# Two interleaved transformer layers on one core: the norm of the one-layer steps behind bank evictions, and the last two feed-forwards' gates by 128-row weights loaded anew

## The chip, the cores and the metric

The kernel runs on one core of one Trainium2 chip. The metric is the device time of one execution in microseconds. TensorE is called PE below, VectorE DVE, ScalarE ACT, GpSimdE POOL; SP is the engine whose queue issues nearly all DMAs.

## The reference, cut to what matters

```python
# x: 1 x 2048 x 448 (bf16); 16 heads of 256; segments of 32 tokens behind 8 memory rows; F = 1792
def A(x, mem):                        # memory-augmented attention, segment after segment
    for s in range(64):
        h = concat([mem, x[:, 32*s:32*s+32]])            # 40 rows
        q, k, v = h @ Wq, h @ Wk, h @ Wv
        p = softmax(mask(q @ k.T * 256 ** -0.5))
        o = (p @ v) @ Wo
        mem = o[:, :8]; outs.append(o[:, 8:])            # the next segment needs this memory
    return concat(outs)

def B(x, W_gate, W_up, W_down):       # gated feed-forward
    return (relu(x @ W_gate) * (x @ W_up)) @ W_down

x = x + A(layernorm(x)); x = x + B(layernorm(x))         # layer 1
x = x + A(layernorm(x)); x = x + B(layernorm(x))         # layer 2, the same weights
```

The segments of a layer are a chain through the memory; the two layers overlap with a lag.

## The kernel before, in words

At the start the kernel fuses the attention weights: `A_sb`, `A3`, `A3z` hold the query-key product, `B_sb` the value-output product. The first dimension of `A_sb` that is sliced is the 128-row part `kd` (0 to 2), the second the half `hf` of the heads (0, 1). Then come 68 steps, `step(g, ff)`. Layer 1 is at segment g, layer 2 at segment g - 4. So steps 0 to 3 have only layer 1 (one chain), steps 4 to 63 both, steps 64 to 67 only layer 2.

Within a step PE runs in an order written out by hand (`in_order` ties every matmul to the one before it): `pairs` and `wide` make the query-key projections of a bank (`prj`), `close_bank` and `leave_bank` copy a bank out to `TQ` or `TZ` on DVE or ACT, `scores_m` and `scores_x` make scores (`Sm`, `Sx`) for memory and token rows, the `weights_` functions the softmax (`mx`, `se`, `ssum`, `rs`, into `PM`, `PX`), `weigh_m`, `weigh_m_rows` and `weigh_x` weigh the rows (`ya`, `yb`, `ym`, `y` into `Y` and `Z`), and `project_out` and `project_tail` project them (`ox`, `o`). `hk` are the transposed rows of the step. Other engines are ordered by a scheduler from the program's text; `tc.keep_in_program_order` pins an instruction to its place in the text among the pinned ones of its engine. There are seven PSUM banks under the tag `ps`, and one under `ox`.

Every odd step from 3 on also carries a feed-forward, `Feed(i)`, of 64 tokens of layer 1 and 64 of layer 2 (block i). It goes through `residual` (adds the attention's output to `xa` and takes the row statistics: `stats`, `mv` on DVE, then `rstd` on POOL), `norm` (`xn`, two DVE instructions that need `rstd`), `xposed` (four transposes into `tps`, one DVE copy to `xT`) and `xposed_rest` (two ACT copies that put the other halves' rows into `xT`), `gate_up(u)` for u = 0 to 6, `down`, and `leave` (the last sum and the output's DMA). Only half of a block is filled in the first (`Feed(0)`, in step 3) and in the last two: `Feed(32)` in step 67, and `end = Feed(33)`, which follows it at the end of the kernel.

`gate_up` keeps the weights in `Wgu_sb` with rows of `W_up` in partitions 0 to 63 and rows of `W_gate` in 64 to 127; the 448 rows make 7 passes of 64. One matmul of 64 rows for up (`ups`) and one for gate (`gps`) run side by side. Each u makes two tiles of 128 columns; ACT copies `ups` to `ut` (two buffers), DVE makes `hh = max(gps, 0) * ut`. `down` multiplies `hh` by `Wd_sb` into `dps`. In the last step the tokens are projected by `project_tokens` (tile `ot`) and added by `add_tokens` (tiles `sums0`, `sums1`), and the last down is made in two column halves (`down_halves`), so that the first half's output leaves while the second is made.

`load_behind` issues a DMA on SP that waits for the last PE instruction in the text so far; `load_piece` uses it to fill `Wgu_sb` and `Wd_sb` early in the run. `mm` (line 83), `tr` (line 86) and `evac` (lines 102, 103) record most matmuls, transposes and copies, so many rows of the profile have these lines, and go by tiles.

Of the kernel before, what the change touches and what calls it, by code (L numbers as in the profile page):

```python
# [54 lines left out]
def build_kernel(ctx, tc, A_x, A_mem0, A_Wq, A_Wk, A_Wv, A_Wo, B_W_gate, B_W_up, B_W_down, out,  # L55
# [16 lines left out]
    last_pe = [None]  # L72
# [20 lines left out]
    def load_behind(dst, src):  # L93
# [4 lines left out]
        return d  # L98

# [342 lines left out]
    hh = main.tile([P, FT, 128], BF, name="hh")  # L442
    part = main.tile([P, 2, DM], F32, name="part")


    class Feed:


        def __init__(self, i):
# [6 lines left out]
            self.both = self.first and self.second  # L456

# [13 lines left out]
        def xposed(self):  # L471
            tps = transpose_tokens(self.xn)
            nc.vector.tensor_copy(xT[:, 0:4, self.n], tps[:, :, self.n])
            return tps

        def xposed_rest(self, tps):
            for r in range(2):
                nc.scalar.copy(xT[ROWS[r], 4:NPASS, self.n], tps[ROWS[1 - r], 0:3, self.n])
# [15 lines left out]

        def down(self):
            i = self.i
            dps = self.dps = [psum.tile([P, 512], F32, tag="ps", name="dps") for _ in range(1 if self.both else 2)]
            for f in range(FT):
                if self.both:
                    mm(dps[0][:, 0:DM], hh[:, f, :], Wd_sb[:, f, :], start=(f == 0), stop=(f == FT - 1))  # L500
                else:
                    mm(dps[f % 2][ROWS[f % 2], 0:DM], hh[:, f, self.n], Wd_sb[:, f, :], start=(f < 2), stop=(f >= FT - 2))
# [7 lines left out]
        def sum_up(self, dst, o):  # L510
# [5 lines left out]
            nc.scalar.copy(part[n, 1, :], self.dps[1 - mine][ROWS[1 - mine], 0:DM])  # L516
# [5 lines left out]
        def down_halves(self):  # L522
            n = self.n
            dps = [[psum.tile([P, 512], F32, tag="ps", name="dps") for _ in range(2)] for _ in range(2)]
            for h, fs in ((0, range(12)), (1, range(6)), (0, range(12, FT)), (1, range(6, FT))):
                d = slice(HALF * h, HALF * h + HALF)
                for f in fs:
                    mm(dps[h][f % 2][ROWS[f % 2], 0:HALF], hh[:, f, n], Wd_sb[:, f, d], start=(f < 2), stop=(f >= FT - 2))
# [130 lines left out]
    def weights_end(se, dst, tag):  # L659
# [7 lines left out]
        nc.vector.tensor_tensor(dst[:, :, 0:L], se, rs.unsqueeze(2).to_broadcast([P, n, L]), op=ALU.mult)  # L667
# [29 lines left out]
    def step(g, ff):  # L697
# [190 lines left out]
        if last:  # L888
            nc.gpsimd.tensor_copy(hb[ROWS[0], j, 4 * HI:4 * HI + 104], hb[ROWS[0], j, 3 * HI:3 * HI + 104])
            begun = [begin_x(hf, scores_x(hf)) for hf in range(2)]  # L890
# [5 lines left out]
            end = Feed(ff.i + 1)  # L896
            project_tokens(0, o[0], 0, 0, NT)
# [3 lines left out]
            px1 = flipped_rows([(PX[1], 2)], "x1")  # L901
            project_tokens(0, o[0], 1, 14, NT)
# [185 lines left out]
```

## Time and profile before

| | before |
|---|---|
| time, median of 3 runs | 1538.44 us (1534.18 to 1540.04) |
| the profiled execution | 1537.08 us, span 1535.3 us |
| PE busy | 1514.6 us, 99% of the span |
| DVE busy | 1048.2 us, 68% |
| ACT busy | 806.3 us, 53% |
| granted PE clock | 0.999 |
| DMA | 33.08 MB; queues at work in the first 5% of the span, mean 22 GB/s over all of it |

The page's shares are taken over the whole span. Steps 3, 65, 66 and 67 take some 70 us of it, so a share says little of them; the timeline of each does. In a timeline a line has the start and the length in us, the engine, the source line, the operation, its output and inputs, the shape and the number merged; in brackets the idle time of that engine before it, and the instruction whose end ended it. Lengths of matmuls overlap, since they are pipelined: the time from one start to the next is their pace.

### The profile page before, as it was taken

How to read it: one execution, taken by the hardware profiler on the slowest of the kernel's cores; microseconds unless marked ns; L12 is line 12 of the kernel's file. 1: busy time of each engine (PE TensorE's matmuls, PEld its weight loads, DVE VectorE, ACT ScalarE, POOL GpSimd, SP SyncE). 2: the span in 40 equal slices, each digit the busy share in tenths (PEclk: the TensorE clock that was granted, in tenths of full speed). 3: DMA queues.
4: the chain of work that ended last, by engine and by line, in shares of the span. 5: the costliest groups of instructions: out<-in, count | busy, mean ns of one | idle time of the engine just before them, and what ended most of it. 6: DMA issues, size and time to landing. Idle time of an engine off the chain costs nothing.

```text
span 1535.3 us, 97340 instructions
## 1 busy us (share of the span) xinstructions
PE 1514.6 (99%) x44691; PEld 1400.5 (91%) x44691; DVE 1048.2 (68%) x3793; ACT 806.3 (53%) x2364; POOL 163.6 (11%) x309
## 2 busy tenths in 40 slices
PE   9999999999999999999999999999999999999998
PEld 6588999999999999999999999999999999999987
DVE  6756767766667667666676676666766776667665
ACT  5645554555455555554555555545555555455534
POOL 4000111011001110110011101100111011011100
PEclk9999999999999999999999999999999999999999
DMA  8910000000000000000000000000000000000000
GB/s 251 243 35 9 9 10 10 5 10 10 10 10 10 10 10 4 10 10 10 10 10 10 9 4 11 10 10 10 10 10 10 5 10 10 10 9 7 7 7 7
DMA packets 29546, 33.08 MB, mean 22 GB/s; under 512 B 3464, under 2 KB 28240, under 8 KB 29136
## 3 DMA queue, kind: packets, MB, share of 16 engines
q1 hardware_dynamic: 28928, 26.74, 6.5%
q8 instruction: 349, 5.72, 1.5%
q14 instruction: 61, 0.50, 0.1%
q10 hardware_dynamic: 144, 0.11, 0.1%
q0 software_dynamic: 64, 0.01, 0.0%
HBM read 23.18 MB, written 1.84 MB: 16 GB/s over the span
## 4 chain that ended last, share of the span: by engine, by line
PE 95%; DVE 2%; DMA 1%; ACT 1%; issue 1%; POOL 0%; DVEq 0%; ACTq 0%
PE prj L83 31%; PE ox L83 25%; PE ups L83 10%; PE dps L83 6%; PE o L83 5%; PE y L83 4%; PE Sx L83 3%; PE aps L83 1%; PE Sm L83 1%; PE pps L86 1%; PE gps L83 1%; PE bps L83 1%; PE tps L86 1%; PE flip L86 1%; PE ym L83 1%; PE tpw L86 1%
## 5 line engine op out<-in xcount | busy, mean ns | idle before, releaser
L83 PEld LDWEIGHTS <-B_sb 128*128 128x128 bf16 (+1 forms) x15008 | 482.6, 103 | 25.5 <-issue 17.9
L83 PE MATMUL prj<-hT,A_sb 128*128 128x80 bf16 (+1 forms) x11256 | 429.1, 200 | 0.0
L83 PEld LDWEIGHTS <-A_sb 128*128 128x128 bf16 x11256 | 406.3, 100 | 7.5
L83 PE MATMUL ox<-Y,B_sb 128*128 128x80 bf16 (+2 forms) x5712 | 218.4, 200 | 0.7 <-ACT Y L765 0.3
L83 PE MATMUL ox<-Z,B_sb 128*128 128x80 bf16 (+1 forms) x5544 | 213.0, 200 | 0.8 <-ACT Z L765 0.8
L83 PE MATMUL ups<-xT,Wgu_sb 64*128 64x128 bf16 (+1 forms) x3332 | 190.0, 213 | 1.5 <-DVE hh L492 0.7
L83 PE MATMUL gps<-xT,Wgu_sb 64*128 64x128 bf16 (+1 forms) x3332 | 190.2, 213 | 1.3 <-issue 0.7
L83 PEld LDWEIGHTS <-Wgu_sb 64*128 64x128 bf16 x6664 | 178.0, 94 | 6.1 <-issue 3.8
L102 ACT CAST TQ<-prj 128x480 bf16<-128x480 f32 (+3 forms) x414 | 175.8, 469 | 13.6 <-PE prj L83 2.0
L103 DVE CAST TQ<-prj 128x480 bf16<-128x480 f32 (+3 forms) x353 | 137.8, 425 | 62.6 <-PE prj L83 62.6
L102 ACT CAST Z<-y 64x128 bf16<-64x128 f32 (+2 forms) x263 | 91.3, 373 | 139.9 <-PE y L83 88.1
L102 ACT CAST TZ<-prj 64x320 bf16<-64x320 f32 (+2 forms) x292 | 110.8, 387 | 78.0 <-PE prj L83 74.6
L491 ACT CAST ut<-ups 128x256 bf16<-128x256 f32 (+1 forms) x238 | 85.3, 359 | 83.0 <-PE gps L83 62.8
L492 DVE SCALAR_TENSOR_TENSOR hh<-gps,ut 128x256 bf16<-128x256 f32 (+1 forms) x238 | 94.1, 407 | 46.9 <-ACT ut L491 34.5
L102 ACT CAST Y<-y 128x512 bf16<-128x512 f32 (+1 forms) x252 | 87.4, 375 | 61.7 <-DVE Y L103 58.7
L102 ACT COPY hT<-tps 128x256 bf16<-128x256 bf16 (+1 forms) x32 | 11.8, 369 | 192.8 <-DVE hT L103 192.8
L103 DVE CAST Y<-y 128x512 bf16<-128x512 f32 (+1 forms) x252 | 102.4, 417 | 9.2 <-ACT Y L102 3.9
L103 DVE CAST Z<-y 64x128 bf16<-64x128 f32 (+2 forms) x257 | 101.7, 417 | 9.7 <-ACT Z L102 4.6
L656 ACT ACTIVATE se<-se 128x80 f32<-128x80 f32 (+2 forms) x270 | 69.6, 292 | 45.2 <-DVE se L655 43.2
L83 PE MATMUL dps<-Wd_sb,hh 128*128 128x448 bf16 (+2 forms) x490 | 90.9, 348 | 0.0
L664 DVE TENSOR_REDUCE ssum<-se 128x2 f32<-128x80 f32 (+2 forms) x270 | 68.3, 267 | 33.0 <-ACT se L656 31.9
L192 POOL TENSOR_SCALAR rstd<-mv 128x1 f32<-128x1 f32 x67 | 15.2, 226 | 696.4 <-DVE mv L190 696.3
(141 smaller groups left out, 2211.6 us busy)
## 6 DMA issues: line engine op xcount, KB each, us to landing
wo<-in_A_Wo_dram SPq DMA_DIRECT2D x8, 448.0 KB, 7.7
Wgu_sb<-in_A_Wq_dram SPq DMA_DIRECT2D x8, 384.0 KB, 5.8
Wgu_sb<-in_A_Wk_dram SPq DMA_DIRECT2D x8, 384.0 KB, 5.8
nat<-in_A_Wv_dram SPq DMA_DIRECT2D x8, 384.0 KB, 5.5
xa<-in_A_x_dram SPq DMA_DIRECT2D x32, 56.0 KB, 2.2
xa<-xp SPq DMA_DIRECT2D x32, 56.0 KB, 1.9
out_dram<-xa SPq DMA_DIRECT2D x31, 56.0 KB, 2.0
xp<-in_A_x_dram SPq DMA_DIRECT2D x30, 56.0 KB, 2.2
```

Source lines behind the costliest of these rows:

```text
L83: in_order(nc.tensor.matmul(*a, **k))
L86: in_order(nc.tensor.transpose(*a))
L102: return nc.scalar.copy(dst, src)
L103: return eng.tensor_copy(dst, src)
L192: nc.gpsimd.tensor_scalar(out=rstd[:], in0=mv[:, 1:2], scalar1=EPS, scalar2=None, op0=ALU.add)
L491: nc.scalar.copy(ut[:, :, n], ups[:, :, n])
L492: nc.vector.scalar_tensor_tensor(out=hh[:, 2 * u:2 * u + 2, n], in0=gps[:, :, n], scalar=0.0, in1=ut[:, :, n], op0=ALU.max, op1=ALU.mult)
L656: nc.scalar.activation(se, se, AF.Exp, scale=SCALE)
L664: nc.vector.tensor_reduce(ssum, se, axis=AX.X, op=ALU.add)
```

## The change

1. In one-chain steps with a feed-forward (3 and 65) `ff.norm()` moves from before `hk_make` to behind the evictions of bank b3. The DVE copy to `xT` is ordered behind the softmax of `scores_m(0)` (`behind`, an order without a semaphore), and the two ACT copies of `xposed_rest` are pinned, which places both behind the evictions of bank c3.
2. The last two feed-forwards (blocks 32 and 33) make their gates with 128-row weights. Rows 0 to 383 of `W_up` and `W_gate` are loaded once more, into the half 0 of `A_sb`, which nothing reads after the projections of step 66: six DMAs of 448 KB, three in step 66, three in step 67 (`load_late`). The last 64 rows stay in part 3 of `Wgu_sb`, whose two halves hold both matrices; a tile `xz` holds x in one half and zeros in the other, so that a 128-row matmul takes only one of them. Each tile of 128 columns is then 3 + 1 matmuls for up and as many for gate, in groups of four tiles (`gate_up_whole`), first all of up, then all of gate.
3. `xT` needs only rows 0 to 383 then (a DVE copy of three parts); the rest goes to `xz` by two small ACT copies (`xposed_whole`).
4. The copies to `ut`, the products to `hh`, the ACT copy to `part` and the statistics of block 33 are pinned. Block 33's `hh` lies in the other 64 columns of the tile, and its norm moves behind all gates of block 32, with `down` between the two blocks' gates as before.
5. `down_halves` uses the tiles `sums0` and `sums1` instead of `part`.

```diff
+    def behind(r, other):
+        tc.add_manual_dep(r.ins, other.ins.name,
+                          mybir.DependencyInfo(mybir.DependencyClass.NoSync, mybir.DependencyReason.DATA),
+                          reason="order of issue")
...
+    xz = main.tile([P, 2, TB], BF, name="xz")
+    whole = [A_sb[:, kd, 0, :, :].rearrange("p t c -> p (t c)") for kd in range(3)]
+    late = [(whole[kd][:, w * F:w * F + F], src[128 * kd:128 * kd + 128])
+            for kd in range(3) for w, src in enumerate((B_W_up, B_W_gate))]
+
+    def load_late():
+        load_behind(*late.pop(0))
...
-        def xposed(self):
+        def xposed(self, other=None):
             tps = transpose_tokens(self.xn)
-            nc.vector.tensor_copy(xT[:, 0:4, self.n], tps[:, :, self.n])
+            r = nc.vector.tensor_copy(xT[:, 0:4, self.n], tps[:, :, self.n])
+            if other is not None:
+                behind(r, other)
             return tps
-        def xposed_rest(self, tps):
+        def xposed_rest(self, tps, pin=False):
             for r in range(2):
-                nc.scalar.copy(xT[ROWS[r], 4:NPASS, self.n], tps[ROWS[1 - r], 0:3, self.n])
+                i = nc.scalar.copy(xT[ROWS[r], 4:NPASS, self.n], tps[ROWS[1 - r], 0:3, self.n])
+                if pin:
+                    tc.keep_in_program_order(i)
...
+        def xposed_whole(self):
+            tps = transpose_tokens(self.xn)
+            nc.vector.tensor_copy(xT[:, 0:3, self.n], tps[:, 0:3, self.n])
+            for r in range(2):
+                nc.scalar.copy(xz[ROWS[r], r, :], tps[ROWS[r], 3, self.n])
+
+        def gate_up_whole(self, f0):
+            n = self.n
+            fs = range(f0, min(f0 + 4, FT))
+            gps = psum.tile([P, 4, TB], F32, tag="ps", name="gps")
+            ups = psum.tile([P, 4, TB], F32, tag="ps", name="ups")
+            for w, ps in enumerate((ups, gps)):
+                for f in fs:
+                    cols = slice(w * F + f * 128, w * F + f * 128 + 128)
+                    for kd in range(3):
+                        mm(ps[:, f - f0, :], whole[kd][:, cols], xT[:, kd, n], ...)
+                    mm(ps[:, f - f0, :], Wgu_sb[:, 3, f * 128:f * 128 + 128], xz[:, w, :], ...)
+            k = len(fs)
+            ut = p_ut.tile([P, 4, TB], BF, tag="ut")
+            tc.keep_in_program_order(nc.scalar.copy(ut[:, 0:k, :], ups[:, 0:k, :]))
+            tc.keep_in_program_order(
+                nc.vector.scalar_tensor_tensor(out=self.hh[:, f0:f0 + k, n], in0=gps[:, 0:k, :], scalar=0.0,
+                                               in1=ut[:, 0:k, :], op0=ALU.max, op1=ALU.mult))
...
@@ sum_up
-            nc.scalar.copy(part[n, 1, :], self.dps[1 - mine][ROWS[1 - mine], 0:DM])
+            c = nc.scalar.copy(part[n, 1, :], self.dps[1 - mine][ROWS[1 - mine], 0:DM])
+            if not self.first:
+                tc.keep_in_program_order(c)
@@ down_halves (and hh becomes self.hh here and in down)
-                    nc.scalar.copy(part[n, 1, d], dps[h][1][ROWS[1], 0:HALF])
-                    nc.vector.tensor_tensor(part[n, 0, d], dps[h][0][n, 0:HALF], self.x[n, d], op=ALU.add)
-                    nc.vector.tensor_tensor(self.x[n, d], part[n, 0, d], part[n, 1, d], op=ALU.add)
+                    sums = main.tile([P, 3, HALF], F32, tag=f"sums{h}", name="sums")
+                    nc.scalar.copy(sums[n, 1, :], dps[h][1][ROWS[1], 0:HALF])
+                    nc.vector.tensor_tensor(sums[n, 0, :], dps[h][0][n, 0:HALF], self.x[n, d], op=ALU.add)
+                    nc.vector.tensor_tensor(self.x[n, d], sums[n, 0, :], sums[n, 1, :], op=ALU.add)
@@ step, the last one
+            load_late()
             begun = [begin_x(hf, scores_x(hf)) for hf in range(2)]
...
             end = Feed(ff.i + 1)
+            load_late()
             project_tokens(0, o[0], 0, 0, NT)
...
             px1 = flipped_rows([(PX[1], 2)], "x1")
+            load_late()
             project_tokens(0, o[0], 1, 14, NT)
...
-            tps = ff.xposed()
+            ff.xposed_whole()
             project_tokens(1, o[1], 1, 14, NT)
-            ff.xposed_rest(tps)
             add_tokens(1, o[1], end.x)
-            end.st = row_stats(end.x)
-            for u in range(FT // 2):
-                ff.gate_up(u)
-                if u == 3:
-                    end.norm()
+            end.hh = hh[:, :, TB:P]
+            end.st = row_stats(end.x, True)
+            for f in range(0, FT, 4):
+                ff.gate_up_whole(f)
+            end.norm()
             ff.down()
-            end.xposed_rest(end.xposed())
+            end.xposed_whole()
             idle(8)
-            for u in range(FT // 2):
-                end.gate_up(u)
-                if u == 0:
+            for f in range(0, FT, 4):
+                end.gate_up_whole(f)
+                if f == 0:
                     ff.leave()
             end.down_halves()
@@ step, all others
         if ff is not None:
             ff.residual()
-            ff.norm(nc.gpsimd if len(chains) == 2 else None)
+            if len(chains) == 2:
+                ff.norm(nc.gpsimd)
...
         close_bank(b3, cs, hb, j, nc.vector, parts=(slice(2, 3), slice(0, 2), slice(3, 5)))
+        if ff is not None and len(chains) == 1:
+            ff.norm()
...
-            tps = ff.xposed()
+            tps = ff.xposed(last_dve[0])
...
-            ff.xposed_rest(tps)
+            ff.xposed_rest(tps, True)
...
+        if len(cs) > len(chains):                 # step 66 alone
+            nc.gpsimd.memset(xz[:], 0.0)
+            load_late()
         project_out(0, 0, 23)
...
         project_tail()
+        if len(cs) > len(chains):
+            load_late()
         project_out(1, 0, 16)
+        if len(cs) > len(chains):
+            load_late()
```

More of the change, by code (lines that the diff above doesn't have):

```diff
@@ L456, in __init__ @@
             self.both = self.first and self.second
+            self.hh = hh
         def flip_out(self, two):
@@ L501, in down @@
                 else:
-                    mm(dps[f % 2][ROWS[f % 2], 0:DM], hh[:, f, self.n], Wd_sb[:, f, :], start=(f < 2), stop=(f >= FT - 2))
+                    mm(dps[f % 2][ROWS[f % 2], 0:DM], self.hh[:, f, self.n], Wd_sb[:, f, :], start=(f < 2), stop=(f >= FT - 2))
             if self.first:
```

10 lines of the change are left out of this document (7 added, 3 removed).

## The prediction

> **What bounds the kernel now.** I read the page first (shares of the engines, chain that ended last), then the timeline of the four steps that the change touches.
>
> ```profile
> PE 1514.6 (99%) x44691; PEld 1400.5 (91%) x44691; DVE 1048.2 (68%) x3793; ACT 806.3 (53%) x2364; POOL 163.6 (11%) x309
> PE 95%; DVE 2%; DMA 1%; ACT 1%; issue 1%; POOL 0%; DVEq 0%; ACTq 0%
> ```
>
> PE is the end-setting engine for 95% of the chain. A local edit can win only PE instructions or one of the few places where PE stands still. The change edits steps 3, 65, 66 and 67 of 68; the other 64 keep their instruction streams in the same order. So everything is decided in about 60 us of 1535.
>
> Step 65 (timeline, all engines; start, length, instruction, idle before and its releaser):
>
> ```profile
> 1472.20 0.99 PE L83 MATMUL prj<-hT,A_sb 128*128 128x40 bf16 x33
> 1472.83 0.61 DVE L202 TENSOR_SCALAR xn<-xa,mv,rstd 128x448 bf16<-128x448 bf16 x2 [1.01 <-POOL rstd L193]
> 1473.35 0.85 DVE L103 CAST TQ<-prj 128x48 bf16<-128x48 f32 x4
> 1473.99 0.24 PE L83 MATMUL Sm<-hT,TQ 128*128 128x40 bf16 x3 [0.80 <-DVE TQ L103]
> 1474.83 0.24 ACT L656 ACTIVATE se<-se 128x40 f32<-128x40 f32 x1 [0.92 <-DVE se L655]
> 1475.80 0.42 DVE L473 COPY xT<-tps 128x512 bf16<-128x512 bf16 x1
> 1477.01 0.24 PE L83 MATMUL Sm<-hT,TQ 128*128 128x40 bf16 x3 [0.54 <-ACT TQ L102]
> 1477.20 0.47 ACT L478 COPY xT<-tps 64x384 bf16<-64x384 bf16 x1
> 1477.70 0.37 ACT L765 CAST Z<-ya 128x256 bf16<-128x256 f32 x1
> 1478.12 0.91 PE L83 MATMUL ox<-Z,B_sb 128*128 128x40 bf16 x30 [0.41 <-ACT Z L765]
> ```
>
> The first norm instruction holds DVE for 1.01 us while POOL makes rstd; four bank evictions stand behind it, and PE waits 0.80 for the third of them. PE then waits 0.54 for a bank copy that stands on ACT between the two xT copies, and 0.41 for Z.
>
> Step 67, its two feed-forwards (blocks 32 and 33), before any edit:
>
> ```profile
> 1518.82 0.19 PE L83 MATMUL gps<-xT,Wgu_sb 64*128 64x64 bf16 x1
> 1519.59 0.79 DVE L886 TENSOR_TENSOR xa<-sums,xa 32x224 bf16<-32x224 f32 x2
> 1519.80 0.19 PE L83 MATMUL ups<-xT,Wgu_sb 64*128 64x64 bf16 x1
> 1520.30 0.19 PE L83 MATMUL gps<-xT,Wgu_sb 64*128 64x64 bf16 x1 [0.31 <-ACT ut L491]
> 1520.62 0.62 DVE L188 BATCH_NORM_STATS2 stats<-xa 128x6 f32<-128x448 bf16 x1
> 1522.44 0.61 DVE L202 TENSOR_SCALAR xn<-xa,mv,rstd 128x448 bf16<-128x448 bf16 x2
> 1522.61 1.74 PE L83 MATMUL dps<-Wd_sb,hh 128*64 128x448 bf16 x14
> 1523.63 0.29 DVE L492 SCALAR_TENSOR_TENSOR hh<-gps,ut 128x128 bf16<-128x128 f32 x1 [0.19 <-ACT ut L491]
> 1524.29 0.40 PE L86 MATMUL tps<-ident,xn 128*128 128x128 bf16 x4
> 1524.72 0.29 DVE L473 COPY xT<-tps 128x256 bf16<-128x256 bf16 x1 [0.80 <-PE tps L86]
> 1525.05 0.65 ACT L478 COPY xT<-tps 64x192 bf16<-64x192 bf16 x2
> 1526.67 0.60 DVE L517 TENSOR_TENSOR part<-dps,xa 64x448 f32<-64x448 f32 x1
> 1527.31 0.62 DVE L520 TENSOR_TENSOR xa<-part 64x448 bf16<-64x448 f32 x1
> 1528.58 0.20 PE L83 MATMUL gps<-xT,Wgu_sb 64*128 64x64 bf16 x1 [0.71 <-issue]
> 1529.56 1.53 PE L83 MATMUL dps<-Wd_sb,hh 128*64 128x224 bf16 x28
> ```
>
> Here PE does not set the pace. The gate matmuls of block 33 run from about 1525.0 to 1529.5, 4.5 us, of which 2.9 are matmuls (98 pairs of 29.2 ns, next part). The rest are waits for banks that the ut copy, the gate product (hh) or the residual (part, xa) still hold.
>
> **The 128-row gates: PE work.** Before, each block has 14 column tiles x 7 passes = 98 pairs of 64-row matmuls, up and gate side by side. From 1518.82 to 1519.80 PE started 67 of them without a stop: 0.98/67 x 2 = 29.2 ns a pair. After, each block has 14 x 2 x 4 = 112 matmuls of 128 rows over 64 columns. The trace of before has no such shape; the nearest rows have the same weights with 80 and with 40 columns:
>
> ```profile
> 1460.42 2.63 PE L83 MATMUL ox<-Y,B_sb 128*128 128x80 bf16 x69
> 1502.78 1.89 PE L83 MATMUL ox<-Y,B_sb 128*128 128x40 bf16 x69 [0.15 <-ACT Y L765]
> L83 PEld LDWEIGHTS <-B_sb 128*128 128x128 bf16 (+1 forms) x15008 | 482.6, 103 | 25.5 <-issue 17.9
> ```
>
> Less the last one's 0.2 us, one starts every (2.63-0.2)/68 = 35.7 and every 24.9 ns. Sixty-four columns lie between; in a straight line 31.4, by the streaming of the pairs (also 64 columns) 29.2. I take 29.2: 112 x 29.2 = 3.27 us against 98 x 29.2 = 2.86. By itself the PE work grows by 0.41 us a block (bounds -0.07 and +1.14). Whatever is gained must come from the waits.
>
> A rule speaks against the change. In the rows above a load lasts 103 ns, yet matmuls with new 128x128 weights start every 24.9 ns, so several loads are in flight under matmuls. The Trainium skill, page "TensorE: Matmul & The Clock Gate", section "The mechanism" (Part 3, packing small matmuls), says that a weight load overlaps a running matmul only where it goes to other row groups; 128-row weights leave no other row group. By that rule the sum would be that of the rival on serial loads below; the 24.9 ns contradict it.
>
> **The 128-row gates: the chain behind them.** Four groups (4, 4, 4 and 2 tiles) take the place of seven, each with one ut copy and one product, at these means:
>
> ```profile
> L491 ACT CAST ut<-ups 128x256 bf16<-128x256 f32 (+1 forms) x238 | 85.3, 359 | 83.0 <-PE gps L83 62.8
> L492 DVE SCALAR_TENSOR_TENSOR hh<-gps,ut 128x256 bf16<-128x256 f32 (+1 forms) x238 | 94.1, 407 | 46.9 <-ACT ut L491 34.5
> ```
>
> So DVE spends 3 x 0.41 + 0.29 = 1.5 us on products instead of 7 x 0.29 = 2.0, and four groups need eight banks of seven, so hardly one wait for a bank remains. On before's clock, with block 32's gates starting where they do (about 1518.47, behind the projection, which covers the xT and xz copies):
> - PE: gates until 1521.74 (before about 1522.5).
> - DVE: residual until 1520.38 (1519.59 + 0.79), then the pinned statistics (0.62 and about 0.25 with gaps) until 1521.25, then the products. Two follow at once (1522.07). The third needs its ut copy, which waits for the first product (two ut buffers): 1522.5. The fourth 1522.8.
> - The down matmuls trail the products by two tiles: end about 1523.1.
> - The norm now stands behind all four products on DVE (before, in the middle): 1522.8 + 0.61 = 1523.4. That is the wait that the change adds; PE's transposes wait for it, 0.40, until 1523.85, then the xT copy, 0.27, until 1524.15. Before, that copy ended at 1525.01. Gain 0.86.
> - Block 33's gates: the fourth matmul waits for the first xz copy (each at most half of 0.65; I take 0.22, so a stop of 0.15). 1524.2 + 0.15 + 3.27 = 1527.6. DVE meanwhile: first product 1525.9, part and xa (0.60 + 0.62) 1527.15, the other products 1527.57, 1527.99, 1528.28, each before the down matmuls get to it.
> - The down in halves, 1.53, ends at 1529.1; before, 1529.56 + 1.53 = 1531.1. **Gain 1.95.** The half sums, the output DMA and the 2.9 us to the end stay.
>
> Bounds: 2.6, if the products never bind and the third ut copy doesn't wait; 0.8, at 35.7 ns a matmul (0.73 x 2 later, of which the first partly hides under the products).
>
> **The loads.** Six loads of 448 KB stand in SP's queue, where nothing else follows until block 32's output; each waits for PE to pass a place and for nobody else. Three are in step 66, three in step 67; the last goes off behind these transposes, and its weights are needed by the gate half of the first group, at 1518.47 + 16 x 0.029 = 1518.9:
>
> ```profile
> 1513.66 0.32 PE L86 MATMUL ppr<-ident,PX 64*128 64x64 bf16 x3
> Wd_sb<-in_B_W_down_dram SPq DMA_DIRECT2D x7, 224.0 KB, 2.9
> DMA to landing us min/median/max: 3.5/5.9/10.5
> ```
>
> A 224 KB load with the queues to itself lands after 2.9 us; the other line is all loads into Wgu_sb, issued amid the crowd of the start. Alone, twice the bytes are at most twice that, 5.8: 1514.0 to 1519.8, 0.9 late; more likely 4, as some of the 2.9 is a fixed cost: in time by 0.9. I take nothing, with 0 to 0.9 for the range. The xz memset goes to POOL, busy 11%: nothing.
>
> **The norm behind the evictions, xT copies pinned.** Step 65: b3's matmuls end 18 of 33 into the stretch at 1472.20, so at about 1472.9; the first b3 eviction, no longer behind the norm, ends at 1473.15, and the first Sm starts at 1473.2, not 1473.99. Then it is given back in part. DVE does the norm (0.61) just where Sm's maximum would come; the exp on ACT moves behind the two copies of c2, from 1474.83 to about 1474.9; so the xT copy stays at about 1475.8. The second Sm comes at about 1476.0 instead of 1477.01, since the c3 copies precede both xT copies on ACT. But Z's copy on ACT stands behind the two xT copies (0.47 each, from 1476.22): 1477.2 instead of 1477.70. **Gain 0.5** (0.2 to 0.8, the whole first wait).
>
> Step 3, the same edit without that wait:
>
> ```profile
> 120.60 0.24 PE L83 MATMUL prj<-hT,A 64*128 64x40 bf16 x6 [0.54 <-issue]
> 121.85 0.24 PE L83 MATMUL Sm<-hT,TQ 128*128 128x40 bf16 x3
> 125.53 0.63 PE L83 MATMUL ox<-Z,B_sb 128*128 128x40 bf16 x19 [0.25 <-ACT Z L765]
> ```
>
> Sm starts where PE gets to it anyway. The norm comes later on DVE, exp stands behind c2's copies and both xT copies before Z's: I take a loss of 0.1 (0.3 loss to 0.2 gain).
>
> **Sum.** -1.95 - 0.5 + 0.1 = -2.35 us, 0.15%. The profiled execution took 1537.08: 1534.7 for its like. The median, 1538.44, lies 1.36 above it: **1536.1**. A measurement of this kernel can tell a change from none at about 0.5%, 7.7 us; the three runs alone spread over 5.9.
>
> **Rivals.**
> - Evictions still bind: ACT's sums, DVE's statistics and products keep both blocks at their old pace, and step 65 gives its gain back at Z. For it: 0.71 of the waits in block 33 stands as "issue", whose cause the trace doesn't name. Against: the count of evictions falls from 28 to 16. Time: -0.5, 1537.9.
> - The last weights land late, the slower side. If the last load takes the 10.5 us that a load into Wgu_sb took at worst, it lands at 1514.0 + 10.5 = 1524.5 instead of 1518.9: 5.6 late, 1541.7 in sum. It makes the kernel slower from a landing of 7.3 us on (4.9 + 2.35). Against: the 10.5 was in a crowd.
> - Serial loads: each 128-row matmul pays 103 + 29 = 132 ns, so 112 x 132 = 14.8 us a block, 11.5 more; two blocks, less the 2.35: 1538.44 + 23.0 - 2.35 = 1559.1. Against: the rows with 24.9 ns.
> - The change doesn't do what it says: the pins leave the old order. The built streams have the norm behind b3's four evictions and four products ahead of the second norm, so I give it nothing beyond the first rival.
>
> **How the numbers follow.** Forecast 0.72 (bounds of its terms: -3.6 to -0.6 us); evictions bind 0.13; late weights 0.11, between no change and +3.3; serial loads 0.02; 0.02 for what I don't see. Range: 1538.44 - 3.6 and about 2 for a median of such runs gives 1532.8; upward it takes in the first rival with the same 2 and the nearer half of the late weights, 1540.3. Faster by over 0.5% would need 7.7 us, more than all waits of the four steps: 0.02. Slower: serial loads and a bit of late weights, 0.04. Within: 0.94.
>
> **What would show it.** Right: the first Sm of step 65 with no wait of 0.8 and Z about 0.5 earlier; 112 matmuls a block at 29 to 31 ns, hardly a wait inside a block; last down matmul about 2 us earlier against the projection; loads landed before 1518.9 on this clock. Wrong: a wait of PE on DMA at the first gate group; matmuls at over 36 ns; products that end after the down matmuls want them; a change of over 1 us outside steps 3 and 65 to 67.

## The result, and the profile after

The changed kernel takes 1534.41 us (median of 20 runs, 1531.24 to 1538.51); the kernel before took 1537.74 in 20 runs beside them (1534.09 to 1544.26). The ratio is 0.9977, 95% interval 0.9967 to 0.9987: some 3.3 us (2.0 to 5.1) faster. That is a real difference, though below the 0.5% that the prediction set as its bound. The forecast change was -2.35 us.

The traced execution of after was a long one, 1537.82 us with a span of 1536.0, 0.7 us longer than before's 1535.3. The list of PE's waits over the whole run tells where that sits (columns: waiting tile and line, releaser, us in total, times, longest). Before:

```profile
PE bps L83 <- DMA wo<-in_A_Wo_dram: 1.8, 1, 1.8
PE prj L83 <- issue: 1.2, 3, 0.5
```

After:

```profile
PE bps L83 <- DMA wo<-in_A_Wo_dram: 4.2, 2, 2.3
PE prj L83 <- issue: 2.2, 4, 0.9
```

The first line is the start, where PE waits for the weights to come in: 2.4 us more in this execution, ahead of everything that the change touches. The second has stops in the first steps, of which one in step 3 is taken up again at the end. Step 65 begins 3.45 us later in this trace, so two traces can be compared only from a point that both pass: here from the first transposes of `OT` in step 65 (1469.53 before, 1472.98 after). Over the stretch from that point to the end of the last down, the longest of the same list are, before:

```profile
PE Sm L83 <- DVE TQ L103: 0.8, 1, 0.8
PE Sm L83 <- ACT TQ L102: 0.8, 2, 0.5
PE gps L83 <- issue: 0.7, 1, 0.7
PE ox L83 <- ACT Z L765: 0.4, 1, 0.4
PE gps L83 <- ACT ut L491: 0.3, 1, 0.3
PE tps L86 <- DVE xn L202: 0.2, 1, 0.2
```

and after:

```profile
PE ox L83 <- ACT Z L812: 0.6, 1, 0.6
PE tps L86 <- DVE xn L207: 0.2, 1, 0.2
PE Sm L83 <- ACT TQ L107: 0.2, 1, 0.2
PE ya L83 <- DVE PT L724: 0.2, 1, 0.2
```

Every listed wait of a gate matmul (`gps`) is gone, and so are the waits of `Sm` behind DVE; the wait for Z has grown. Step 65 of after in its timeline:

```profile
1476.31 0.47 DVE L108 CAST TQ<-prj 128x48 bf16<-128x48 f32 x2 [0.44 <-PE prj L83]
1476.57 0.24 PE L83 MATMUL Sm<-hT,TQ 128*128 128x40 bf16 x3
1476.70 0.60 DVE L207 TENSOR_SCALAR xn<-xa,mv,rstd 128x448 bf16<-128x448 bf16 x2
1479.14 0.24 PE L83 MATMUL Sm<-hT,TQ 128*128 128x40 bf16 x3
1479.34 0.96 ACT L494 COPY xT<-tps 64x384 bf16<-64x384 bf16 x2
1480.32 0.37 ACT L812 CAST Z<-ya 128x256 bf16<-128x256 f32 x1
1480.74 0.91 PE L83 MATMUL ox<-Z,B_sb 128*128 128x40 bf16 x30 [0.59 <-ACT Z L812]
```

The evictions stand before the norm, and `Sm` has no bracket any more. From the common point the first `Sm` starts after 3.59 us (before 4.46), the second after 6.16 (7.48), the first `ox` after 7.76 (8.59). Half a microsecond of what the second `Sm` won is given back at Z, which stands on ACT behind 0.96 us of xT copies. Net: 0.83.

Step 67 of after:

```profile
1521.11 0.26 PE L83 MATMUL ups<-xT,A_sb 128*128 128x64 bf16 x3
1524.35 0.19 PE L83 MATMUL gps<-xz,Wgu_sb 128*128 128x64 bf16 x1
1524.48 1.51 PE L83 MATMUL dps<-Wd_sb,hh 128*64 128x448 bf16 x14
1525.04 0.60 DVE L207 TENSOR_SCALAR xn<-xa,mv,rstd 128x448 bf16<-128x448 bf16 x2
1525.92 0.40 PE L86 MATMUL tps<-ident,xn 128*128 128x128 bf16 x4
1526.36 0.26 DVE L515 COPY xT<-tps 128x192 bf16<-128x192 bf16 x1 [0.72 <-PE tps L86]
1526.67 0.25 PE L83 MATMUL ups<-xT,A_sb 128*128 128x64 bf16 x3
1526.91 0.19 PE L83 MATMUL ups<-xz,Wgu_sb 128*128 128x64 bf16 x1
1530.18 1.53 PE L83 MATMUL dps<-Wd_sb,hh 128*64 128x224 bf16 x28
```

Block 32's 112 gate matmuls start from 1521.11 to 1524.35: 3.24/111 = 29.2 ns each. The norm `xn` is ready at 1525.64, 0.28 before the transposes start, which carry no wait. The last down starts at 1530.18. The stage lengths of both kernels, each from its own trace (us; step 67 from the first transposes of `OT` to the end of the last sum on DVE):

| | before | after | difference |
|---|---|---|---|
| step 65, to the first `ox` | 8.59 | 7.76 | -0.83 |
| from there to step 67 | 32.28 | 32.29 | 0 |
| step 67 | 22.01 | 19.99 | -2.02 |
| of it block 32's gates | 4.02 | 3.24 | -0.78 |
| of it block 33's gates | 4.37 | 3.38 | -0.99 |

With 0.16 to 0.26 more in step 3 (below), -2.6 to -2.7 us in sum, inside the interval of the times.

### The profile page after: what moved, and what is told of

The parts are those of the page before. It is cut to its first block, busy times and chain, and to the rows that moved or that the text cites. A ratio compares the mean times of both kernels' runs of the same rounds, so it can differ in the third digit from the quotient of the medians.

```text
span 1536.0 us, 96988 instructions
## 1 busy us (share of the span) xinstructions
PE 1514.6 (99%) x44523; PEld 1401.3 (91%) x44523; DVE 1047.2 (68%) x3787; ACT 804.4 (52%) x2358; POOL 163.8 (11%) x310
## 4 chain that ended last, share of the span: by engine, by line
PE 96%; DVE 1%; DMA 1%; issue 1%; ACT 1%; POOL 0%; SPq 0%; DVEq 0%; ACTq 0%
PE prj L83 31%; PE ox L83 25%; PE ups L83 10%; PE dps L83 6%; PE o L83 5%; PE y L83 4%; PE Sx L83 3%; PE aps L83 1%; PE Sm L83 1%; PE gps L83 1%; PE pps L86 1%; PE bps L83 1%; PE tps L86 1%; PE flip L86 1%; DMA wo<-in_A_Wo_dram 1%; PE ym L83 1%
## 5 line engine op out<-in xcount | busy, mean ns | idle before, releaser
L83 PEld LDWEIGHTS <-A_sb 128*128 128x128 bf16 x11424 | 413.6, 100 | 7.8 <-issue 0.2
L83 PE MATMUL ups<-xT,Wgu_sb 64*128 64x128 bf16 (+1 forms) x3136 | 182.7, 214 | 1.2 <-DVE hh L510 0.9
L83 PE MATMUL gps<-xT,Wgu_sb 64*128 64x128 bf16 (+1 forms) x3136 | 182.9, 214 | 0.0
L509 ACT CAST ut<-ups 128x256 bf16<-128x256 f32 (+1 forms) x224 | 81.7, 365 | 78.5 <-PE gps L83 61.7
L510 DVE SCALAR_TENSOR_TENSOR hh<-gps,ut 128x256 bf16<-128x256 f32 (+1 forms) x224 | 90.2, 414 | 44.3 <-ACT ut L509 32.3
```

The lines of the kernel that those rows point to most:

```text
L83: in_order(nc.tensor.matmul(*a, **k))
L509: nc.scalar.copy(ut[:, :, n], ups[:, :, n])
L510: nc.vector.scalar_tensor_tensor(out=hh[:, 2 * u:2 * u + 2, n], in0=gps[:, :, n], scalar=0.0, in1=ut[:, :, n], op0=ALU.max, op1=ALU.mult)
```

## The experiments

Stage lengths of all kernels, in that manner. A stage repeats to about 0.3 us from one trace to the next, as step 67 of "norm only" against before, whose code is the same there, shows; where that comes from is seen further down. The last four kernels of the table were run once each, so only their traces speak.

| kernel | step 65 | step 67 | gates 32 | gates 33 |
|---|---|---|---|---|
| before | 8.59 | 22.01 | 4.02 | 4.37 |
| after | 7.76 | 19.99 | 3.24 | 3.38 |
| norm only | 7.93 | 22.32 | 4.28 | 4.65 |
| gates only | 8.59 | 20.26 | 3.25 | 3.38 |
| pairs by four | 7.76 | 21.63 | 3.42 | 4.64 |
| 128 rows by two | 7.77 | 20.83 | 3.96 | 3.51 |
| pairs by two | 7.77 | 21.98 | 4.22 | 4.38 |
| pairs by four, late leave | 7.79 | 22.90 | 4.01 | 4.38 |
| Z first | 7.32 | 20.05 | 3.24 | 3.38 |
| pairs by four, 64 transposes more | 7.78 | 22.58 | 4.61 | 3.04 |
| pairs by four, 128 transposes more | 7.77 | 21.43 | 2.95 | 4.67 |
| after, 64 transposes more | 7.77 | 21.69 | 3.24 | 3.39 |
| the same without the loads | 7.76 | 19.98 | 3.25 | 3.38 |

**Each half alone.** "Norm only" is the kernel before with part 1 of the change, whose lines stand above. "Gates only" is the changed kernel with part 1 taken back (this and all further diffs are against the changed kernel).

```diff
-            if len(chains) == 2:
-                ff.norm(nc.gpsimd)
+            ff.norm(nc.gpsimd if len(chains) == 2 else None)
...
-        if ff is not None and len(chains) == 1:
-            ff.norm()
...
-            tps = ff.xposed(last_dve[0])
+            tps = ff.xposed()
...
-            ff.xposed_rest(tps, True)
+            ff.xposed_rest(tps)
```

> Only the first part of the change: in steps 3 and 65 the norm behind b3's evictions, the xT copies ordered and pinned; the last two feed-forwards as before. Lengths are read from the trace: step 65 from its first transpose of OT to its first ox matmul is 8.59 us before and 7.76 after; the last step from its first transpose of OT to the end of the last xa sum is 22.01 before and 19.99 after. Theory (the two parts are independent and add up): step 65 7.8 (7.6 to 7.9), last step 22.0 (21.9 to 22.1), time 0.8 us under before (ratio 0.9995). Rival (the gain of step 65 depends on the later steps, or is a wait that only moved): step 65 8.3 or more, or the last step longer by what step 65 wins.

> Only the second part: the last two feed-forwards with 128-row weights, groups of four, pins and late loads; steps 3 and 65 as before. Theory: step 65 8.6 (8.5 to 8.7), last step 20.0 (19.9 to 20.1), time 2.0 us under before (ratio 0.9987). Rival (loads or pins cost something that the earlier norm hides): last step 20.5 or more.

Norm only: 1537.07 us, ratio 0.9995 (0.998 to 1.0011); its step 65 takes 7.93, so it has that gain and no other. Gates only: 1534.73, ratio 0.9984 (0.997 to 0.9998); step 67 takes 20.26, step 65 is before's 8.59 to the hundredth. The two gains are in two places and add up. Step 67 is in both a little longer than expected (22.32 and 20.26); both times PE stands longer at places where it waits for nothing that the profile shows, which the runs below explain.

**What of the gates wins: the weights' shape, or the groups?** Two kernels make the other two corners: 64-row pairs in after's four groups, pins and order, without the late loads, and 128-row weights in groups of two tiles. A third has pairs by two with after's pins and order.

```diff
 # pairs by four, in gate_up_whole
-            for w, ps in enumerate((ups, gps)):
-                for f in fs:
...
-                    for kd in range(3):
-                        mm(ps[:, f - f0, :], whole[kd][:, cols], xT[:, kd, n], ...)
...
+            for i in range(NPASS):
+                for f in fs:
+                    for r, ps in enumerate((ups, gps)):
+                        mm(ps[:, f - f0, :], Wgu_sb[ROWS[r], i, f * 128:(f + 1) * 128], xT[ROWS[r], i, n], ...)
 # 128 rows by two
-            for f in range(0, FT, 4):
+            for f in range(0, FT, 2):
```

> The changed kernel with its gates made again by 64-row pairs, up and gate side by side, from the weights that lie there: groups of four tiles, pins, the place of the norm and the separate hh stay; no late loads. Theory (the gain came from fewer waits on evictions, and the 128-row weights by themselves cost 0.4 us a block): block 33's gates take 2.9 plus a stop of 0.3 for the xT copies instead of 3.4, block 32 stays bound by DVE: last step 19.8 us (19.5 to 20.1), as good as the changed kernel's 19.99 or better, without the loads. Rival (128-row weights are what made it faster, since all of up comes first and its copy runs under the gate half): evictions come in bunches, last step 20.8 or more.

> The changed kernel with groups of two tiles instead of four: 128-row weights, loads, pins and order stay, but seven ut copies and seven products a block, fourteen banks instead of eight. Theory (the number of evictions decides): DVE's products take 2.0 us a block instead of 1.5 and PE waits for banks again: last step 20.8 us (20.4 to 21.3). Rival (the pins and the order alone decide): last step 20.0 (19.8 to 20.2).

> The fourth corner of a square: 64-row pairs, groups of two tiles as before, but the pins, the late norm, the separate hh and sums tiles of the change; no late loads. Last step, from its first transpose of OT to the end of the last xa sum: before 22.01 us, pairs by four 21.63, 128-row by two 20.83, 128-row by four 19.99. Theory A (shape and grouping each win about what their own corner showed, pins and order nothing): 22.0 to 22.5, as before. Rival B (pins and order win by themselves): 21.5 or less.

Times: pairs by four 1537.6, ratio 0.9996 (0.9981 to 1.001); 128 rows by two 1535.88, 0.9982 (0.9968 to 0.9996); pairs by two 1533.97 beside 1536.62 for before, 0.9986 (0.9972 to 1.0). The times can't part these; step 67 can:

| step 67, us | groups of two | groups of four |
|---|---|---|
| 64-row pairs | 21.98 | 21.63 |
| 128-row weights | 20.83 | 19.99 |

Pins, order and the second `hh` win nothing by themselves (21.98 against before's 22.01). Fewer evictions win 0.84 with the 128-row weights, as expected; with the pairs 0.35, hardly more than two traces of the same code differ. The shape wins 1.15 and 1.64, though by the prediction's own sum it only adds PE work: the expectation that pairs by four need 19.8 us failed by 1.8. That sum isn't wrong: block 32 of "128 transposes more" ran its 98 pairs without a stop in 2.95 us, where the 128-row form takes 3.24. The shape must remove something that the prediction had put down to banks. With groups of two the 128-row form still has a wait for a bank:

```profile
1522.96 0.25 PE L83 MATMUL gps<-xT,A_sb 128*128 128x64 bf16 x3 [0.55 <-DVE hh L536]
```

With groups of four the pairs have none of that sort, but two stops without a releaser (timeline of pairs by four):

```profile
1520.17 0.20 PE L83 MATMUL gps<-xT,Wgu_sb 64*128 64x64 bf16 x1 [0.38 <-issue]
1527.66 0.20 PE L83 MATMUL gps<-xT,Wgu_sb 64*128 64x64 bf16 x1 [1.42 <-issue]
```

**Are these stops a bank that the residual holds?** The residual of block 32 (`leave`) runs on DVE and ACT near the second of them. I moved it from behind block 33's first group to behind its third.

```diff
-                if f == 0:
+                if f == 8:
                     ff.leave()
```

> Pairs by four as in the run before, with block 32's residual (part, xa, its output DMA) behind the third group of block 33 instead of the first. There PE stood 1.6 us in block 33, until the second product, which stood on DVE behind part and xa. Theory A (with pairs both banks of a group are asked for at once, so PE runs into banks that the residual keeps from being released; the 128-row form asks for the gate bank half a group later): the stop goes, block 33's gates 3.2 to 3.6 us instead of 4.64, last step 20.0 to 20.6. Rival B (the shape of the weights itself is needed): gates of block 33 over 4.2, last step 21.2 or more.

The account of banks fell. The residual moved, the stop did not (timeline):

```profile
1518.56 0.20 PE L83 MATMUL gps<-xT,Wgu_sb 64*128 64x64 bf16 x1 [0.96 <-issue]
1525.77 0.20 PE L83 MATMUL gps<-xT,Wgu_sb 64*128 64x64 bf16 x1 [1.15 <-issue]
1528.76 0.48 PE L83 MATMUL dps<-Wd_sb,hh 128*64 128x224 bf16 x6 [0.77 <-DVE hh L532]
```

The third line is the price of the move: the late residual now holds up a product that the last down needs. The time was 1536.01, ratio 1.0005 (0.9992 to 1.0018). What gave the cause away is the place: in all five kernels with pairs so far the stop in block 33 (0.82 to 1.61 us) comes after exactly 137 of its 196 matmuls, by two or by four, whatever stands on DVE and ACT.

**Is it TensorE's instruction stream?** The page has a queue for instructions (packets, MB, share; after):

```profile
q8 instruction: 348, 5.70, 1.6%
```

5.70 MB in 348 packets are 16 KB each. The page counts 44,523 matmuls and as many weight loads on PE, 89,046 instructions: 256 to a packet. Counted through the run, the stops without a releaser of before and of the pairs in step 67 stand at matmul 44,348 or 44,604, two blocks apart. To test it I left step 67 alone and put more idle transposes at the start of the program, so that every later instruction stands half a block (`idle(96)`) or a whole block (`idle(160)`) further on; and the half block also ahead of the changed kernel.

```diff
-        idle(32)
+        idle(96)
         cur = flip_next(0)
```

> The pairs in groups of four, with 64 more idle transposes at the start of the program, so that every later TensorE instruction stands 128 places (64 matmuls, each with its weight load) later in TensorE's stream. If the stops without a releaser are the stream running dry at the edge of a block of 256 instructions, they move: the one in block 33 from after 137 matmuls to after about 73, the one in block 32 from after 103 to after about 39, each again one to two us behind the end of an instruction packet. If they are banks or buffers of that place in the block, they stay after 137 and 103 whatever stands ahead. Step 67 stays within 21 to 22.5 us in both.

> The same with 128 more idle transposes than the pairs by four have, 256 instructions, a whole block: by the stream's account the stops are back where they were, in block 33 after about 137 matmuls and in block 32 after about 103; by the account of banks they are there too. Together with the shift by half a block it tells a period of 256 from a stop that any shift moves: if the stop stands elsewhere here, the block is not of 256 instructions. Step 67 21 to 22.5 us.

> The changed kernel with 64 more idle transposes at the start. The stream's account says that the 128-row form eats a block in 3.7 us, about as fast as one comes, and so has no stop at any place: gates of 3.2 to 3.5 us in both blocks, step 67 in 19.9 to 20.4 us. If instead the changed kernel only had luck with where its blocks' edges fall, a stop of 0.5 to 1.5 us without a releaser shows in one of its two blocks and step 67 takes 20.5 to 21.5 us.

Pairs by four with 64 transposes more (timeline):

```profile
1523.01 0.20 PE L83 MATMUL gps<-xT,Wgu_sb 64*128 64x64 bf16 x1 [1.57 <-issue]
1530.77 1.34 PE L83 MATMUL dps<-Wd_sb,hh 128*64 128x224 bf16 x23 [0.98 <-issue]
```

With 128 more:

```profile
1534.31 0.20 PE L83 MATMUL gps<-xT,Wgu_sb 64*128 64x64 bf16 x1 [1.43 <-issue]
```

With half a block, the stop after 137 matmuls is gone from block 33, whose gates take 3.04 us instead of 4.64. One stands in block 32 instead, after 167, and one in the last down. I had expected them after 73 and 39 matmuls, and step 67 within 22.5 (it took 22.58). There are edges at both places, but PE did not stop there; it stopped at the next edge of the first (39 + 128 = 167) and of the second (73 + 128 = 201, five into the down). An edge alone makes no stop, it needs a block that was eaten too fast. With a whole block the stop is back after 137 matmuls and lasts 1.62 us; the one after 103 is not there this time. Counted through the run all of them, shifted or not, stand 60 beyond a multiple of 128 matmuls (44,476 and 44,732; 44,732). Places that move in the step with the instructions ahead, and come back at 256, are the stream's.

The traces have the packets of that queue one by one. In the last seven blocks of all 14 kernels (98 edges) the packet that an edge needs always started after PE had passed the edge before (0.06 to 3.0 us later) and took 0.9 to 1.4 us. All 19 stops at an edge (over 0.2 us from one matmul's start to the next) ended 1.25 to 1.56 us after the end of their packet. So one block is fetched while the one before is worked off, and a round, from edge to edge, took 2.4 us at the least and 2.9 to 3.7 at the stops of the pairs. The 64-row pairs eat 256 instructions in 128 x 14.6 ns = 1.9 us, the 128-row matmuls of 29.2 ns in 3.7. With groups of four that is what the shape wins: pairs by four stand 0.57 and 1.61 us at two edges, the 128-row form nowhere, for some 0.4 us more of PE work a block. With groups of two it is only part of it: pairs by two stand 0.82 at an edge, and the rest of their loss are gaps behind copies and products (`ut`, `hh`, `xT`), 2.2 us together against 1.1 in the 128-row form; why these shrink with the shape was not tested. Before's "issue" in block 33, 0.91 us between matmuls at edge 44,604, is the stream. "Norm only", 0.31 longer in step 67, stands 0.85 and 1.19 us at edges 44,348 and 44,604, where before stands 0.28 and 0.91.

The Trainium skill, page "Runtime: NRT & Kernel Launch", section "Instruction fetch mechanics", says that an engine's instructions come in 16 KiB blocks of 256, fetched while the current block runs, and that this is mostly hidden. The blocks agree with the 256 counted here; "mostly hidden" holds for before from 171 us to step 67, where one stop over 0.2 us is found, but not in the gates, where stops of 0.3 to 1.8 us are measured, nor in the first steps (last section).

**The loads, and the same shift on the changed kernel.** After with 64 transposes more took 21.69 in step 67, not 20. Its gates have no stop, as expected; the stops are in the projections ahead of them, at matmuls 44,092 and 44,220:

```profile
1513.80 0.93 PE L83 MATMUL ot<-B_sb,Z 128*32 128x224 bf16 x29 [0.56 <-issue]
1519.30 1.61 PE L83 MATMUL ot<-B_sb,Z 128*32 128x224 bf16 x57 [0.91 <-issue]
```

Here the packets started 2.15 and 3.04 us after the edge before; in the kernels with pairs, which load nothing late, 0.3 to 1.6 at the same two edges. The six late loads of 448 KB run just then. So the same kernel without them, in which the 128-row gates multiply what `A_sb` still holds:

```diff
     def load_late():
-        load_behind(*late.pop(0))
+        late.pop(0)
```

> The changed kernel with 64 more idle transposes at the start, and without its six late loads: the 128-row gates multiply what A_sb still holds, so the last 128 tokens of the output are other numbers; the instructions of TensorE are the same. With the loads, TensorE stood in the projections of step 67 at two edges of its instruction blocks (0.56 and 0.91 us without a releaser), and the instruction packet behind each of them started 2.15 and 3.04 us after TensorE had passed the edge before, when the packets of the loads had ended. If the loads hold up the instruction packets, those packets now start 0.8 to 1.6 us after the edge, as in the kernels by pairs, which have no such loads; both stops are gone, the gates of block 32 start at 8.0 to 8.4 us of step 67 instead of 9.78, and the step takes 19.9 to 20.4 us instead of 21.69. If the place of the edge alone makes the stops, they stay, and the step takes 21 us or more.

The packets started 0.91 and 0.50 us after the edge, both stops are gone, and step 67 took 19.98. So the loads hold up the fetch of instructions, here at a price of 1.7 us. The traced execution of after has the 19.99 of the kernel without loads, but that isn't a property of its edges alone. Five kernels have the loads without a shift; the packet for edge 44,092 started 1.00 (after), 2.20 (Z first), 2.22 (128 rows by two), 2.50 (gates only) and 2.69 us (late load) after the edge before, and PE's next matmul came 0.01, 0.17, 0.11, 0.38 and 0.65 us after its last. The gates of block 32 start 8.07 or 8.08 us into the step in all eight kernels without loads, and 8.07 to 8.63 in these five.

**A late load.** The last load goes off later, behind all 112 projection matmuls of step 67 instead of behind the first 42.

```diff
             px1 = flipped_rows([(PX[1], 2)], "x1")
-            load_late()
...
             project_tokens(1, o[1], 1, 14, NT)
+            load_late()
```

> The changed kernel with its last load (the third part of W_gate) put behind block 32's transposes instead of behind the transposes of the last weighing: it goes off some 3.8 us later. Prices the rival of late weights. The loads land 3.2 to 5.1 us after issue in the changed kernel. Theory A (the gate half of the first group waits until it lands, and the chain behind has no slack): last step 22.3 to 23.5 us instead of 19.99. Rival B (the products of block 32 bind, and hide most of a late gate): 21 or less.

1539.34 us, ratio 1.0014 (1.0002 to 1.0025): a little slower than before. In its timeline:

```profile
1516.10 0.33 SPq L94 DMA_DIRECT2D A_sb<-in_B_W_gate_dram  x1
1519.87 0.20 PE L83 MATMUL gps<-xT,A_sb 128*128 128x64 bf16 x1 [2.38 <-DMA A_sb<-in_B_W_gate_dram]
```

Step 67 took 24.63, more than either expectation: 4.64 longer for a wait of 2.38. Most of the rest is the clock (by stretch: length, busy time of PE, PEld, DVE, ACT and POOL, then the granted PE clock, the DMA share and GB/s):

```profile
1519.80:1520.00 0.20, 0.13 (x5) 0.14 (x6) 0.00 (x0) 0.00 (x0) 0.20 (x1) 1.00 0.00 0
1520.00:1521.00 1.00, 1.00 (x28) 1.00 (x27) 0.42 (x1) 0.00 (x0) 0.33 (x1) 0.66 0.00 0
1521.00:1522.00 1.00, 1.00 (x23) 1.00 (x21) 0.00 (x0) 0.37 (x1) 0.00 (x0) 0.50 0.00 0
1522.00:1523.00 1.00, 1.00 (x23) 1.00 (x21) 0.42 (x1) 0.00 (x0) 0.00 (x0) 0.50 0.00 0
1523.00:1524.00 1.00, 1.00 (x28) 1.00 (x26) 0.03 (x1) 0.37 (x1) 0.00 (x0) 0.63 0.00 0
1524.00:1525.00 1.00, 1.00 (x20) 0.69 (x17) 0.96 (x4) 0.27 (x1) 0.00 (x0) 1.00 0.06 16
```

From 1520 to 1524 the clock granted 2.29 of 4 us, 1.71 lost. The remaining 0.55 stands ahead of the wait: it is the stop of 0.65 at edge 44,092, by which the gates of block 32 start 8.63 us into the step instead of 8.07.

**Z first.** What is left in step 65 is the wait for Z. Its copy goes ahead of both xT copies on ACT: they are ordered behind it by the new third argument.

```diff
-        if ff is not None and len(chains) == 1:
-            ff.xposed_rest(tps, True)
...
-            weigh_m(0, hk, pm)
+            first = weigh_m(0, hk, pm)
+            if ff is not None:
+                ff.xposed_rest(tps, True, first)
```

> The changed kernel with the two xT copies of steps 3 and 65 behind the copy of ya to Z on ACT. In the changed kernel ox of step 65 waits 0.59 us for that copy, which stands behind both xT copies (0.48 each). Theory A (ACT's order is all that holds Z): step 65, first transpose of OT to first ox, 7.1 to 7.4 us instead of 7.76, and the gates behind lose nothing. Rival B (the wait moves to the gates' last passes, which then wait for xT): step 65 shorter, but step 65 to step 67, 32.29 us from the first ox to the first transpose of OT, longer by as much. Time: 0.5 us under the changed kernel, too little for the times to tell.

```profile
1476.47 0.27 PE L83 MATMUL ya<-PT,hk 128*128 128x128 bf16 x2 [0.17 <-DVE PT L726]
1476.78 0.37 ACT L814 CAST Z<-ya 128x256 bf16<-128x256 f32 x1 [0.58 <-PE ya L83]
1477.17 0.47 ACT L494 COPY xT<-tps 64x384 bf16<-64x384 bf16 x1
1477.20 0.91 PE L83 MATMUL ox<-Z,B_sb 128*128 128x40 bf16 x30
```

`ox` has no bracket, step 65 takes 7.32 instead of 7.76, and the xT copies are still in time (32.28 to step 67). 1533.58 us, ratio 0.9976 (0.9961 to 0.9992) against before: the best version by step 65 of its trace, 0.4 under after there, which the times can't show.

## Why the prediction was right, and where it was not

- **Sum and range.** Forecast -2.35 us and 1536.1; measured 1534.41, inside the range, and 3.3 below the longer series of before. By the traces the steps gave -2.6 to -2.7.
- **PE work of the 128-row gates.** Right: 29.2 ns a matmul was taken, 29.2 measured, and the pairs without a stop took 2.95 and 3.04 us against 3.24 to 3.38. Serial loads at 132 ns are refuted. The rule of the Trainium skill behind them (page "TensorE: Matmul & The Clock Gate", section "The mechanism": a load overlaps a matmul only in other row groups) does not hold for this shape. The same section also lets a load be pulled ahead where it goes to a background weight buffer; the 29.2 ns are at odds with the first and not with the second.
- **"Whatever is gained must come from the waits."** Right in size, wrong in a good part of the cause. The step that failed is "the rest are waits for banks that the ut copy, the gate product or the residual still hold". Of block 33's 1.6 us of gaps (start to start), 0.91 was one stop of the instruction stream, 0.46 stood behind the two ACT copies to `xT`, and only 0.22 behind a product and the residual. In block 32 the `ut` copy and a product had 0.83, the stream 0.28, an `xT` copy 0.10. Grouping, which the step credits with the gain, is worth 0.35 to 0.84; the shape, which it priced as a loss, 1.15 to 1.64. That the sum came out is luck in this part: the same reasoning gave 19.8 us to the pairs by four, which took 21.63. The first rival had its finger on this: it named the 0.71 of "issue" without a cause. It fell all the same, since the new shape removes that stop too.
- **Block 33 starts earlier.** Taken 0.86, measured 1.0 from the transposes' start (12.89 us into the step, before 13.89). "The wait that the change adds", the norm behind four products, did not bind: `xn` was ready 0.28 before the transposes started, without a wait, behind the down. The short stop for the first `xz` copy was taken at 0.15; the fourth matmul of block 33 starts 0.24 after the first instead of 0.09, so 0.15.
- **Last down 1.95 earlier.** Measured 2.01 (17.15 us into the step, before 19.16).
- **Loads at nothing.** Right for the traced execution of after: landings 3.2, 4.3 and 5.1 us (least, median, most), the last issued at 1516.66, its gates at 1521.58 without a wait. But the sum saw a load only as something that lands late. It also holds up the instruction packets, for 1.7 us in the shifted kernel and for up to 0.56 in the four others with the same edges, so it was luck that this cost nothing in the execution that was traced.
- **Late weights.** It did not happen; the experiment shows that the rival was priced too low: 2.38 us late cost 4.1, not 2.38, and the halved clock is the reason (the other 0.55 of the 4.64 stands ahead of the wait).
- **Step 65.** 0.83 against 0.5, at the end of the range given (0.2 to 0.8). The second `Sm` came 1.32 earlier where 1.0 was taken, and the return at Z was as described.
- **Step 3.** A loss of 0.1 taken. From its first `Sm` to the first `ox` the old order took 3.68 us in both kernels that have it, the new 3.83 to 3.94 in nine of the eleven that have it with Z last: 0.16 to 0.26. The traced execution of after is one of the other two, with 4.57: its matmuls ran at half clock there (last section). The second, pairs by four with 64 transposes more, took 4.48 with a stop of 0.67 at a block's edge in this stretch, at 122.51 us.

## What to carry to other kernels

Where TensorE works through many small matmuls, count its instructions as well as its nanoseconds: here 256 of them (128 matmuls with new weights) can't pass in less than the 2.4 to 3.7 us that the next block takes to come, and a form with little more than half as many (112 matmuls for 196) wins although it is slower on the array. A stop without a releaser that stays at the same instruction while its neighbours move is to be tested by shifting the program by half a block before any bank or buffer is blamed. A large late load should be priced twice, as data that may be late and as traffic ahead of the instruction packets, and one trace is not enough for the second price: it was 0 to 0.56 us in five kernels with the same edges.

## What the runs showed of the hardware that I had not expected

- The fetch of instructions, above: 2.4 us from edge to edge at best, 2.9 to 3.7 at the stops of the pairs, up to 5.5 under the loads. It costs more in the first steps than in the last one. Before has six more such stops between 78 and 171 us, 3.1 us together, each ending 1.2 to 1.5 us after a packet; the `prj` of step 3 that the prediction shows with 0.54 of "issue" is one. Their matmul counts leave 95 to 92 over a multiple of 128, against 60 at the end of the run; the slow fall would be instructions other than matmuls and their loads, which I did not trace. Over the 14 traces the stops of that kind between 60 us and the last 1500 matmuls add up to 1.8 to 7.0 us, beside the some 3 us that the change wins.
- A wait of 2.38 us was enough to halve the granted clock, not at once but some 0.45 us after work had begun again, for 3.4 us (the 0.66 and the 0.63 read as parts of a stretch at half speed). The traced execution of after has the same in step 3, after a stop of only 0.89 us on `prj` at 123.75, which is at a block's edge too, in a step in which PE has other gaps (same columns):

```profile
125.00:126.00 1.00, 1.00 (x38) 1.00 (x36) 1.00 (x7) 0.62 (x4) 0.00 (x0) 0.57 0.08 16
126.00:127.00 1.00, 1.00 (x28) 1.00 (x26) 0.34 (x2) 0.70 (x5) 0.00 (x0) 0.50 0.00 0
127.00:128.00 1.00, 1.00 (x29) 0.97 (x27) 0.60 (x4) 0.39 (x4) 0.00 (x0) 0.50 0.00 0
128.00:129.00 1.00, 0.97 (x20) 0.75 (x18) 0.80 (x6) 0.94 (x5) 0.00 (x0) 0.72 0.00 0
```

Again 3.4 us at half speed. The Trainium skill, page "TensorE: Matmul & The Clock Gate", section "What's actually happening", has a clock that is either full or half and a window of about 3.4 us; the 0.50 and the 3.4 us agree. By the same section an idle window of 3.4 us slows it; here a single gap of 2.38 us, and gaps of which the longest was 0.89, came before it. The stops of up to 1.8 us in step 67 of the pairs had no such consequence, nor had a stop of 0.89 on the same `prj` in pairs by four, so what decides stays open. One thing more is in the clock records of the 14 traces: between two changes the full clock lasts a whole multiple of 3.413 us (10.24, 61.44 and 1450.66 are 3, 18 and 425 of them), so the clock changes on a fixed grid of that length, and a change comes at the next point of it and not a fixed time after a gap.
